# Strassen's seven products for the first MLP layer of the last eight token tiles, and other places for the scores of batches 6 and 7

## The chip, the cores and the metric

One core of a Trainium2 chip. The metric is the time of one execution in device microseconds (us), lower is better. The kernel before took 570.96 us (median of 3 runs, 569.7 to 571.33).

## What is computed

Cosine attention of 8 batches, 12 heads, 448 tokens, 64 channels a head, then a mixer: a low-rank mixing along the tokens and a two-layer MLP, each with its residual.

```python
q_n = q / (norm(q) + 1e-6);  k_n = k / (norm(k) + 1e-6)
attn = softmax(q_n @ k_n.T / tau)
x = (attn @ v), heads side by side          # 8 x 448 x 768
u = x + ((x.T @ U) @ V).T                   # rank 32, along the tokens
out = u + relu(u @ w_ch1) @ w_ch2           # 768 -> 3072 -> 768
```

All inputs and the output are float32; the kernel multiplies in bf16 and accumulates in fp32.

## The kernel before

**Tiles.** The 3584 tokens are 28 tiles of 128. The MLP takes them in order: five units of 3 or 4 tiles (`UNITS`, units 0 to 4, together 16 tiles) by `mlp` (L1085), then the last 12 tiles in six pairs (pairs 0 to 5) by `mlp_seven` (L995). Attention of later batches runs between the matmuls of earlier units. `u` is made per batch in `stage0` (L833); its transpose uT, with channels on the partitions, comes by DMA transposes on SP's queue (`columns_of`, L792).

**A unit.** First layer: for each of 24 blocks of 128 hidden units, six matmuls with a block of w1 as weights and uT as moving data (L1098), into one bank; a ReLU on ACT or DVE (L1121, L1123) writes bf16. Second layer: for each tile and half of the columns, 24 matmuls (L1134), then DVE adds u (L1145), and SP stores the rows.

**A pair.** Its first layer is direct: 12 times two blocks of w1, six matmuls of 256 columns each (L1007), both into one bank, and a ReLU of 512 (L1017, L1019). After every three of the twelve, four DVE sums of 384 (L1029 to L1033) make the combinations of ReLU blocks that Strassen's algorithm (in Winograd's form) needs: S1, S2, S4 and one in place. The second layer then is seven products instead of eight: each 12 matmuls of 384 columns (L1042) with blocks of ReLU, or of their sums, as weights, and blocks of w2, or of their sums, as moving data. The sums of w2 are made once, in `seven_weights` (L965), on DVE (L976). Products share banks and are read in the middle of their accumulation: product 1 is copied out by ACT (L1062); POOL adds three quarters of u to that copy (L1064); DVE adds a bank to such a sum (L1057). Products run in the order 1, 6, 2, 7, 5, 4, 3. A product that goes on in a bank waits for the sum that reads it.

**What sets the order.** Every instruction is an `Op` with an engine, an assumed duration, what it depends on, and the buffers that it acquires and releases (`Slot`, `Ring`; PSUM's eight banks as `BankRing`). `Plan.run` (L156) plays these out with the assumed durations and issues the instructions in the order that results. PE's work lies in streams of fixed order; ACT, DVE and SP take what is ready, by priority; POOL has one queue. On the chip each engine runs its list in this order and waits on semaphores. Where the plan has a gap on PE of more than 0.25 us, it fills it with matmuls on a warm-up tile.

**The scores.** From batch 2 on, scores of a batch come in seven bursts of three (L677): six matmuls on PE (L695; the first burst has twelve of half size), then three exponentials on ACT (L713); `values` (L719) follows as exponentials end. A burst is tied to a place among the matmuls of the MLP: batch b + 2 to the second layer of unit b (`SPOTS`, L1149 to L1154), batch 7 to seven places in pairs 0 and 1 (near L1315). The first burst of a batch needs the transposed keys and queries (qkT) of all six pairs of heads; these come by DMA transposes on SP (L649) into six buffers that the batch before frees burst by burst.

Of the kernel before, what the change touches and what calls it, by code (L numbers as in the profile page):

```python
# [11 lines left out]
FP = mybir.dt.float32  # L12
BF = mybir.dt.bfloat16
AF = mybir.ActivationFunctionType
# [255 lines left out]
def kernel(  # L270
# [12 lines left out]
    nc = tc.nc  # L283

    B, H, S, D = q.shape
    C = H * D
    R = moe_U.shape[-1]
    F = moe_w_ch1.shape[-1]
    NPAIR = H // 2
    CC = C // 128  # L290
    NC = F // 128
    CH = C // 2
    SC = 4
    SCH = S // SC
# [12 lines left out]
    const = ctx.enter_context(tc.tile_pool(name="const", bufs=1))  # L307
# [5 lines left out]
    def fixed(n, shape, dt, name):  # L313

        tiles = [const.tile(shape, dt, name=f"{name}{i}") for i in range(n)]
        return tiles

    def ring(n, shape, dt, name, space=None):
        p = space or pool
        return Ring(n, lambda i: p.tile(shape, dt, name=name, tag=name, bufs=n))  # L320

    def fixed_ring(tiles):
        return Ring(len(tiles), lambda i: tiles[i % len(tiles)])

    HF, QC = NC // 2, 2 * G * SC * D
# [1 line left out]
    ld_t = [qk_t[0:SCH, QC * i:QC * (i + 1)].rearrange("p (i h x) -> p i h x", i=2, h=G) for i in range(3)]  # L327
    xn_t = [qk_t[0:SCH, 3 * QC + 1024 * i:3 * QC + 1024 * (i + 1)].rearrange("p (c x) -> p c x", c=2 * SC)
            for i in range(3)]
    attn_t = fixed(3, [128, SC, 2, 512], BF, "attn")  # L330
    tail_t = [t_[:, SC - 1] for t_ in attn_t]
    v_t = fixed(2, [128, H, SC, D + 8], BF, "v_nat")

# [3 lines left out]
    r_ss = ring(4, [SCH, 2, G, SC], FP, "ss")  # L337
    r_ln = ring(4, [SCH, 2, G, SC], FP, "ln")
    r_inv = ring(4, [SCH, 2, G, SC], FP, "inv")
    r_qkT = ring(6, [128, 2 * SC, SCH], BF, "qkT")  # L340
    r_X = ring(2, [128, 4, C], BF, "X_sb")
    r_A = ring(3, [128, C], BF, "A_sb")
    u_t = const.tile([128, 8, C], BF, name="u_nat")
    r_u = fixed_ring([u_t[:, i, :] for i in range(8)])
# [23 lines left out]
    lead = First()  # L368
    O_t = fixed(3, [128, CH], FP, "O_sb")
    r_O = fixed_ring(O_t)  # L370
    spare = [uT_t[:, CC * 256:].bitcast(FP), relu_t[:, 84 * 128:].bitcast(FP)]
    r_O2 = fixed_ring([x[:, CH * i:CH * (i + 1)] for x in spare for i in range(2)] + O_t)
    r_rd = ring(2, [128, 4, 1], FP, "rd")
    bank_t = psum.tile([128, 8, 512], FP, name="bank")
    banks = Banks(8)
# [1 line left out]
    def bank_ring(groups, cap, shape=None):  # L377
        def make(g):
            if len(g) > 1:
                return bank_t[:, g[0]:g[-1] + 1, :]  # L380
            t_ = bank_t[:, g[0], :]
            if shape is not None:
                t_ = t_[:, 0:shape[0] * shape[1]].rearrange("p (a b) -> p a b", a=shape[0])
            return t_
        return BankRing(banks, groups, cap, make)
# [12 lines left out]
    r_scb = bank_ring([(0, 1), (2, 3)], 2)  # L398
    r_out = bank_ring([(7,), (6,), (5,), (4,)], 4)
    r_warm = bank_ring([(4,)], 1)  # L400
    r_sc1 = bank_ring([(0,), (2,), (1,), (3,)], 4)


# [34 lines left out]
    def pe_t(n):  # L438
        return n / 2400.0 + 0.0025
# [7 lines left out]
    def any_t(n, fast=1, fixed=0.065):  # L447
        return {"ACT": act_t(n), "DVE": dve_t(n, fast, fixed)}
# [333 lines left out]

    class Columns:

        def __init__(self, n):
            self.slot, self.n = Slot(r_uT, NC * CC), n

        @property
        def tile(self):
            return self.slot.tile[:, 0:CC * self.n].rearrange("p (c n) -> p c n", c=CC)  # L790

    def columns_of(tiles):  # L792

        uT = Columns(128 * len(tiles))
        us, ut = [], []
        for i, x in enumerate(tiles):
            u, adds = made[x]
            us.append(u)
            ut.append(plan.add(Op("SP", 0.1, lambda i=i, u=u: nc.sync.dma_start_transpose(
                out=uT.tile[:, :, i * 128:(i + 1) * 128], in_=u.tile),  # L800
                deps=adds, acq=[uT.slot], rel=[u], prio=0, lat=("x", 0.05 * 48, 2.0))))
        return us, uT, ut
# [145 lines left out]
    def store(tile_, c0, c1, O, o):  # L948

        z, t = tile_  # L950
        w = c1 - c0
        for bb in (2 * z, 2 * z + 1):
            o0 = (bb % 2) * S
            lo, hi = max(128 * t, o0), min(128 * (t + 1), o0 + S)
            if lo >= hi:
                continue
            for nn, j, p0, p1 in segments(lo - o0, hi - o0):
                r0 = nn + o0 - 128 * t
                O.uses += 1
                O.left += 1  # L960
                plan.add(Op("SP", 0.1, lambda bb=bb, j=j, p0=p0, p1=p1, r0=r0: nc.sync.dma_start(
                    out=rows(out[bb], j, p0, p1)[:, c0:c1], in_=O.tile[r0:r0 + p1 - p0, 0:w]),
                    deps=[o], rel=[O], prio=2, lat=("x", (p1 - p0) * w * 4 / 200e3, 2.0)))

    def seven_weights(after, qk_free, v_free):  # L965

# [25 lines left out]
                 6: lambda j: T2[:, j], 7: lambda j: B_[:, j, 0, 1]}  # L992
        return right, by

    def mlp_seven(tiles, right, made_by):  # L995

        us, uT, ut = columns_of(tiles)
        rl = relu_t.rearrange("p (x t) -> p x t", t=128)
        Q = rl[:, 0:4 * HF].rearrange("p (j x) t -> p j x t", x=4)
        S1, S2, S4 = [rl[:, 4 * HF + HF * i:4 * HF + HF * (i + 1)] for i in range(3)]  # L1000
        relu = Slot(r_relu, 7)
        tops, ready = [], {}
        for j in range(HF):
            mm = Slot(r_up, 1)
            for e in range(2):
                for cc in range(CC):
                    o = plan.add(Op("PE", pe_t(256), lambda j=j, e=e, cc=cc, mm=mm: nc.tensor.matmul(  # L1007
                        out=mm.tile[:, 256 * e:256 * e + 256], lhsT=w1_sb[:, cc, (2 * j + e) * 128:(2 * j + e + 1) * 128],
                        rhs=uT.tile[:, cc, :], start=(cc == 0), stop=(cc == CC - 1)),
                        deps=ut if cc == 0 else [], acq=[mm] if cc == 0 and e == 0 else [], rel=[uT.slot]), pe_mlp)  # L1010
            tops.append(o)
            r = Op("ACT/DVE", any_t(512), None, deps=[o], acq=[relu], rel=[mm], prio=0)

            def fn(r=r, j=j, mm=mm):
                dst = rl[:, 4 * j:4 * j + 4].rearrange("p x t -> p (x t)")
                if r.by == "ACT":
                    nc.scalar.activation(out=dst, in_=mm.tile[:, 0:512], func=AF.Relu)  # L1017
                else:
                    nc.vector.tensor_relu(out=dst, in_=mm.tile[:, 0:512])  # L1019
            r.fn = fn  # L1020
            ready[j] = {1: plan.add(r)}
            ready[j][2] = ready[j][4] = ready[j][1]
            if j % 3 == 2:
                x = slice(j - 2, j + 1)
                t = 0.06 + 384 * 0.00053

                def sums(f, deps):
                    return plan.add(Op("DVE", t, f, deps=deps, acq=[relu], prio=0.1))
                a = sums(lambda x=x: nc.vector.tensor_add(S1[:, x], Q[:, x, 1], Q[:, x, 3]),  # L1029
                         [ready[i][1] for i in range(j - 2, j + 1)])  # L1030
                c = sums(lambda x=x: nc.vector.tensor_sub(S2[:, x], S1[:, x], Q[:, x, 0]), [a])
                d = sums(lambda x=x: nc.vector.tensor_sub(S4[:, x], Q[:, x, 2], S2[:, x]), [c])
                e_ = sums(lambda x=x: nc.vector.tensor_sub(Q[:, x, 1], Q[:, x, 0], Q[:, x, 1]), [a])  # L1033
                for i in range(j - 2, j + 1):
                    ready[i].update({3: d, 5: a, 6: c, 7: e_})
        left = {1: lambda j: Q[:, j, 0], 2: lambda j: Q[:, j, 2], 3: lambda j: S4[:, j], 4: lambda j: Q[:, j, 3],
                5: lambda j: S1[:, j], 6: lambda j: S2[:, j], 7: lambda j: Q[:, j, 1]}
        line = []
# [1 line left out]
        def product(k, mm, first, last, deps=()):  # L1040
# [5 lines left out]
                    acq=[mm] if first and j == 0 else [], rel=[relu] if j == HF - 1 else []), pe_mlp)  # L1046
            line.append(o)
            return o
        a, b, c = Slot(r_mm, 1), Slot(r_mm, 1), Slot(r_mm, 1)
        s1, y12, y22, y21, o11 = Slot(r_O2, 3), Slot(r_O2, 0), Slot(r_O2, 0), Slot(r_O2, 0), Slot(r_O2, 0)  # L1050
        u1, u2 = us

        def dve(f, deps, acq=(), rel=()):
# [5 lines left out]
        def tile_of(s):  # L1059
            return lambda: s.tile  # L1060
        p1 = product(1, a, True, False)
        cp = plan.add(Op("ACT", 0.42, lambda: nc.scalar.copy(out=s1.tile, in_=a.tile[:, 0:CH]),  # L1062
                         deps=[p1], acq=[s1], prio=-0.5))
        y = [plan.add(Op("POOL", 1.0, lambda y_=y_, u=u, c0=c0: nc.gpsimd.tensor_add(  # L1064
            out=y_.tile, in0=s1.tile, in1=u.tile[:, c0:c0 + CH]), deps=[cp], acq=[y_], rel=[s1, u]), pool_q)
            for y_, u, c0 in ((y12, u1, CH), (y22, u2, CH), (y21, u2, 0))]
        p6 = product(6, b, True, False)
        z12 = dve(bank(tile_of(y12), tile_of(y12), b), [p6, y[0]])
        p2 = product(2, a, False, True, [cp])
# [15 lines left out]
    def mlp(b, tiles, us, uT, ut):  # L1085
# [62 lines left out]
                store(t, c0, c1, O, o)  # L1148

        last_down[b] = [x[-1] for x in downs]  # L1150
        todo = bursts.get(b + 2, ()) if b else ()
        for o, f in zip(bursts.get(2, ()) if b == 1 else (), [0,3,6,9,12,15,18,21]):
            o.deps.append(tops[f])
        spots = [(g, f) for g in range(len(downs)) for f in SPOTS[len(downs)][g]] if todo else ()  # L1154
# [150 lines left out]
    for b, tiles in enumerate(UNITS):  # L1305
# [2 lines left out]
    seven = seven_weights(last_down[len(UNITS) - 1],  # L1308
                          [o for p in range(NPAIR) for o in got[B - 1, p, "qkT"][1]],
                          [last_av[B - 2, p] for p in range(NPAIR)])  # L1310
    hosts = []
    for n in range(0, len(rest), 2):
        hosts.append(mlp_seven(rest[n:n + 2], *seven))
    (t0, l0), (t1, l1) = hosts[:2]
    for o, at in zip(bursts[B - 1], (t0[2], t0[7], l0[0], l0[3], t1[2], t1[7], l1[0])):  # L1315
        o.deps.append(at)

    order = plan.run()
# [44 lines left out]
```

## Time and profile before

| what | value |
|---|---|
| median of three runs | 570.96 us (569.7 to 571.33) |
| the profiled execution, whole | 571.55 us |
| its span, first to last instruction | 569.0 us |
| granted TensorE clock over the span | 0.997 |
| pair 2: first layer, second layer | 15.72 us, 13.65 us |
| L1007, 864 matmuls of 256 columns | 97.6 us busy |
| L1042, second layer of the pairs | 504 matmuls of 384 columns |
| L713, 163 exponentials of 896 | 917 ns each |
| DVE busy, 448 to 569 us | 34.3 of 121 us |
| ACT busy, 448 to 569 us | 30.6 of 121 us |

The profile is one execution. In the view of groups the duration of a matmul includes its way through the array (273 ns for 256 columns), while the next one starts 109 ns later; so lengths of stretches are taken from the chain, and single durations only for the other engines. Start to start is less than the duration on DVE, ACT and POOL too. Lines of the form "start, length, engine, line, operation, out<-in" come from the timeline, with what an engine waited for in square brackets.

### The profile page before, as it was taken

What the parts mean: (1) busy time and instruction counts of PE and PEld (TensorE: products, weight loads), DVE (VectorE), ACT (ScalarE), POOL (GpSimd) and SP (SyncE); (2) the same over time, 40 slices, a digit from 0 to 9 for tenths busy, and PEclk for the clock granted to TensorE, in tenths of its full rate; (3) what the DMA queues carried; (4) which work ended last, traced back from release to release, by engine and by line L of the source; (5) the groups of instructions that cost most, each with busy time, mean ns of one, the idle gap of its engine ahead of it and who ended that gap; (6) DMA issues with size and microseconds to landing.
All of it is one profiled execution on the core that took longest, in us unless ns stands there. A gap on an engine that the chain in (4) does not pass through costs nothing.

```text
span 569.0 us, 12604 instructions
## 1 busy us (share of the span) xinstructions
PE 559.8 (98%) x5207; PEld 362.1 (64%) x5207; DVE 337.8 (59%) x815; ACT 284.5 (50%) x472; POOL 118.1 (21%) x162
## 2 busy tenths in 40 slices
PE   8899999999999999999999999999999999999997
PEld 6565566544565565566556655686786777777784
DVE  7889969987674786477437722479444532323232
ACT  6876645577525672666555546446263231313140
POOL 7626142060041105002300400002001010101001
PEclk9899999999999999999999999999999999999999
DMA  9999999794769649684957714311203111311201
GB/s 152 203 208 136 210 196 137 82 151 76 121 79 151 92 67 113 106 116 52 108 107 131 53 26 85 77 31 31 54 4 43 43 29 56 29 55 29 57 1 55
DMA packets 132665, 50.51 MB, mean 89 GB/s; under 512 B 97760, under 2 KB 132608, under 8 KB 132608
## 3 DMA queue, kind: packets, MB, share of 16 engines
q0 software_dynamic: 72352, 25.73, 40.2%
q1 hardware_dynamic: 60256, 23.98, 21.6%
q8 instruction: 40, 0.66, 0.5%
q14 instruction: 17, 0.14, 0.1%
HBM read 52.02 MB, written 11.01 MB: 111 GB/s over the span
## 4 chain that ended last, share of the span: by engine, by line
PE 94%; DVE 3%; DMA 1%; ACT 1%; issue 0%; POOL 0%; DVEq 0%; ACTq 0%; POOLq 0%
PE bank L1134 22%; PE bank L1098 22%; PE bank L1007 17%; PE bank L1042 14%; PE bank L740 8%; PE bank L695 6%; PE bank L895 2%; DMA qk_all<-in_k_dram 1%; PE bank L488 1%; DVE qk_all L634 1%; ACT attn L708 1%; PE bank L845 1%; DVE X_sb L771 0%; DVE ss L566 0%; DVE ln L586 0%
## 5 line engine op out<-in xcount | busy, mean ns | idle before, releaser
L713 ACT ACTIVATE attn<-bank 128x896 bf16<-128x896 f32 (+1 forms) x163 | 139.2, 917 | 71.7 <-PE bank L695 66.6
L1134 PE MATMUL bank<-w_sb,relu 128*128 128x384 bf16 x768 | 136.3, 326 | 0.0
L1098 PE MATMUL bank<-uT,w_sb 128*128 128x384 bf16 (+1 forms) x720 | 135.3, 337 | 0.0
L1134 PEld LDWEIGHTS <-relu 128*128 128x128 bf16 x768 | 71.0, 98 | 53.4 <-issue 10.7
L1098 PEld LDWEIGHTS <-w_sb 128*128 128x128 bf16 x720 | 67.3, 98 | 54.4 <-issue 6.7
L1007 PE MATMUL bank<-uT,w_sb 128*128 128x256 bf16 x864 | 97.6, 273 | 0.0
L1007 PEld LDWEIGHTS <-w_sb 128*128 128x128 bf16 x864 | 83.8, 98 | 12.4 <-issue 1.8
L1017 ACT ACTIVATE relu<-bank 128x512 bf16<-128x512 f32 x68 | 40.6, 597 | 100.5 <-PE bank L1007 100.5
L1042 PEld LDWEIGHTS <-relu 128*128 128x128 bf16 x504 | 48.7, 98 | 32.4 <-issue 1.4
L1121 ACT ACTIVATE relu<-bank 128x384 bf16<-128x384 f32 (+1 forms) x84 | 42.7, 509 | 48.2 <-PE bank L1098 47.7
L566 DVE TENSOR_REDUCE ss<-sq_all 112x8 f32<-112x512 bf16 x96 | 61.9, 672 | 5.4 <-ACT sq_all L558 5.0
L740 PEld LDWEIGHTS <-attn 128*128 128x128 bf16 (+1 forms) x1536 | 55.0, 98 | 9.1 <-issue 3.5
L634 DVE TENSOR_TENSOR qk_all<-qk_all,inv 112x512 bf16<-112x512 bf16 x93 | 60.7, 680 | 0.1
L740 PE MATMUL bank<-v_nat,attn 128*128 128x65 bf16 (+1 forms) x1536 | 58.1, 194 | 0.8 <-DVE X_sb L771 0.4
L1042 PE MATMUL bank<-w_sb,relu 128*128 128x384 bf16 x288 | 50.4, 326 | 0.0
L1145 DVE TENSOR_TENSOR O_sb<-bank,u_nat 128x384 f32<-128x384 f32 x32 | 17.7, 555 | 51.9 <-PE bank L1134 47.6
L695 PE MATMUL bank<-qkT 64*128 64x448 bf16 (+1 forms) x384 | 47.3, 357 | 1.1 <-ACT qkT L1160 0.5
L510 POOL DMA_DIRECT2D qk_all<-in_q_dram x24 | 17.5, 730 | 141.8 <-ACT attn L713 51.9
L533 POOL DMA_DIRECT2D v_nat<-in_v_dram x42 | 31.0, 744 | 68.7 <-PE bank L740 40.3
L771 DVE TENSOR_TENSOR X_sb<-bank,rd 128x256 bf16<-128x256 f32 x96 | 39.2, 417 | 1.8 <-DVE rd L769 0.2
L1029 DVE TENSOR_TENSOR relu<-relu 128x384 bf16<-128x384 bf16 x24 | 8.6, 357 | 52.5 <-ACT relu L1017 52.3
L558 ACT ACTIVATE sq_all<-qk_all 112x512 bf16<-112x512 bf16 x53 | 31.1, 629 | 7.6 <-DVE ss L566 7.6
(96 smaller groups left out, 419.6 us busy)
## 6 DMA issues: line engine op xcount, KB each, us to landing
qk_all<-in_q_dram POOLq DMA_DIRECT2D x23, 224.0 KB, 5.2
qk_all<-in_k_dram POOLq DMA_DIRECT2D x23, 224.0 KB, 5.8
w_sb<-in_moe_w_ch_dram POOLq DMA_DIRECT2D x4, 1152.0 KB, 17.4
w_sb<-in_moe_w_ch_dram POOLq DMA_DIRECT2D x8, 576.0 KB, 15.8
out_dram<-O_sb SPq DMA_DIRECT2D x14, 168.0 KB, 2.3
v_nat<-in_v_dram POOLq DMA_DIRECT2D x11, 168.0 KB, 7.9
out_dram<-O_sb SPq DMA_DIRECT2D x12, 144.0 KB, 2.1
out_dram<-O_sb SPq DMA_DIRECT2D x11, 120.0 KB, 2.1
```

What stands on the lines that cost most here:

```text
L566: lambda i=i, a0=a0, a1=a1, sq=sq: nc.vector.reduce_sum(ss.tile[:, i, a0:a1, :].rearrange("p h c -> p (h c)"), sq.tile[:, 0:a1 - a0, :].re ...
L634: nc.vector.tensor_mul(dst, src, sc)
L695: nc.tensor.matmul(out=out, lhsT=qkT.tile.rearrange("p b s -> p (b s)")[r, n0:n0 + w], rhs=qkT.tile[r, SC:2 * SC, :].rearrange("p c s -> p ...
L713: exps.append(plan.add(Op("ACT", act_t(2 * S, 0.08), lambda sc=sc, c=c, attn=attn: nc.scalar.activation(out=attn.tile[:, :, off:off + S] i ...
L740: nc.tensor.matmul(out=av.tile[:, t, 0:D + 1], lhsT=tail.tile[:, hh, 128 * t:128 * (t + 1)] if tail and j == SC - 1 else (attn if j < SC - ...
L771: muls.append(plan.add(Op("DVE", dve_t(256), lambda av=av, rd=rd, h=h: nc.vector.tensor_mul(X.tile[:, :, h * D:(h + 1) * D], av.tile[:, :, ...
L1007: o = plan.add(Op("PE", pe_t(256), lambda j=j, e=e, cc=cc, mm=mm: nc.tensor.matmul(out=mm.tile[:, 256 * e:256 * e + 256], lhsT=w1_sb[:, cc ...
L1017: nc.scalar.activation(out=dst, in_=mm.tile[:, 0:512], func=AF.Relu)
L1042: o = plan.add(Op("PE", pe_t(CH), lambda j=j: nc.tensor.matmul(out=mm.tile[:, 0:CH], lhsT=left[k](j), rhs=right[k](j), start=(first and j ...
L1098: o = plan.add(Op("PE", pe_t(n), lambda cc=cc: nc.tensor.matmul(out=mm.tile[:, 0:n], lhsT=w1_sb[:, cc, f * 128:(f + 1) * 128], rhs=uT.tile ...
L1121: nc.scalar.activation(out=relu.tile[:, f, 0:n], in_=mm.tile[:, 0:n], func=AF.Relu)
L1134: nc.tensor.matmul(out=mm.tile[:, 0:c1 - c0], lhsT=relu.tile[:, f, i * 128:(i + 1) * 128], rhs=w2_t[:, f, c0:c1], start=(f == 0), stop=(f ...
```

## The change

**First layer of pairs 2 to 5** (`up_seven`). uT of the pair is split into 2 x 2 (channels, tokens) and w1 into 2 x 2 (channels, hidden units); seven products replace eight. A product is 12 hidden blocks x 3 channel blocks of 128 columns. The blocks lie in three groups of four; a group fills one bank of 512. The products run in the order 1, 6, 2, 7, 5, 3, 4, each over all three groups. Per group: ACT copies product 1 out of its bank; product 2 goes on in that bank, and ACT's ReLU reads it; DVE adds the bank of 6, and of 6 + 7, to the copy, then the banks of 5, 5 + 3 and 6 + 7 + 4 to these; ReLUs of the three that lie in SBUF run on ACT (two) and DVE (one). Four sums of 384 on DVE make the columns' combinations. `sums_of` then makes S1, S2, S4 and the sum in place by groups of 512, S4 of the first two groups on POOL.

**Rows of w1** (`seven_rows`). Twelve DVE sums of 1536, once, into the memory of attention tiles and qkT, which therefore must be done with batch 7; three of the twelve are in place in w1 and wait for the last first-layer matmul of pair 1.

**Second layer of pairs 2 to 5.** The order is 1, 4, 6, 5, 7, 2, 3, with four banks instead of three.

**Scores.** Bursts of batch 6 and 7 get places listed by hand, in both layers of unit 4 and in pair 0.

**Buffers.** The attention tiles, qkT and X_sb become one tile each, cut into views; the spare memory in uT is no longer an output buffer.

```diff
-    attn_t = fixed(3, [128, SC, 2, 512], BF, "attn")
+    attn_all = const.tile([128, 3 * AT], BF, name="attn")
...
-    spare = [uT_t[:, CC * 256:].bitcast(FP), relu_t[:, 84 * 128:].bitcast(FP)]
+    spare = relu_t[:, 84 * 128:].bitcast(FP)
...
+    r_mm4 = bank_ring([(7,), (6,), (5,), (4,), (3,), (2,), (1,), (0,)], 4)
+    r_pure = bank_ring([(7,), (6,), (5,), (4,), (3,), (2,), (1,), (0,)], 8)
...
+    def seven_rows(after, free):
...
+        for i in range(3):
+            A11, A12, A21, A22 = A_[:, i, 0, :, 0], A_[:, i, 1, :, 0], A_[:, i, 0, :, 1], A_[:, i, 1, :, 1]
+            a = rows_(lambda o=S1[i], x=A21, y=A22: nc.vector.tensor_add(o, x, y), free)
+            c = rows_(lambda o=S2[i], x=S1[i], y=A11: nc.vector.tensor_sub(o, x, y), [a])
+            d = rows_(lambda o=S4[i], x=A12, y=S2[i]: nc.vector.tensor_sub(o, x, y), [c])
+            e = rows_(lambda o=A21, x=A11, y=A21: nc.vector.tensor_sub(o, x, y), [a, *after])
+            by[i] = {3: d, 5: a, 6: c, 7: e}
...
+    def up_seven(tiles, relu, tops, ready, left, made_by, x_free):
...
+        a = cols_(lambda: nc.vector.tensor_sub(T(0), U()[:, :, 0, 1], U()[:, :, 0, 0]), ut)
+        c = cols_(lambda: nc.vector.tensor_sub(T(1), U()[:, :, 1, 1], T(0)), [a])
+        d = cols_(lambda: nc.vector.tensor_sub(T(2), U()[:, :, 1, 0], T(1)), [c])
+        e = cols_(lambda: nc.vector.tensor_sub(U()[:, :, 0, 1], U()[:, :, 1, 1], U()[:, :, 0, 1]), [a])
...
+        def product(k, g, mm, first, deps=()):
+            for j in gs[g]:
+                for i in range(3):
...
+                    o = plan.add(Op("PE", pe_t(128), lambda i=i, j=j, jj=jj: nc.tensor.matmul(
+                        out=mm.tile[:, 128 * jj:128 * jj + 128], lhsT=left[k](i, j), rhs=right[k][0](i),
...
+        for k in (1, 6, 2, 7, 5, 3, 4):
+            for g in range(len(gs)):
+                A, B_, C_ = banks_of[g]
...
+                if k == 1:
+                    o = product(1, g, A, True)
+                    x["cp"] = op("ACT", 0.57, lambda g=g, A=A: nc.scalar.copy(out=s1[g].tile, in_=A.tile[:, 0:512]),
...
+                elif k == 6:
+                    o = product(6, g, B_, True)
+                    x["z12"] = op("DVE", PS, sum_op(of(z12[g]), of(s1[g]), B_, False), [o, x["cp"]], [z12[g]])
...
+                elif k == 7:
+                    o = product(7, g, B_, False, [x["z12"]])
...
+                elif k == 5:
+                    o = product(5, g, C_, True)
+                    x["q22"] = op("DVE", PS, sum_op(blocks(g, 3), wide(z22[g]), C_, True), [o, x["z22"]], [relu], [z22[g]])
...
+                elif k == 3:
+                    o = product(3, g, C_, False, [x["q22"]])
...
+                    sums_of(gs[g], relu, ready, [x["r11"]], [x["r12"]], [x["r21"]], [x["r22"]], "POOL" if g < 2 else "DVE")
...
+    def sums_of(js, relu, ready, r11, r12, r21, r22, by="DVE"):
...
+        a = sums(lambda: nc.vector.tensor_add(S1[:, x], Q[:, x, 1], Q[:, x, 3]), [*r12, *r22])
+        c = sums(lambda: nc.vector.tensor_sub(S2[:, x], S1[:, x], Q[:, x, 0]), [a, *r11])
+        e_ = sums(lambda: nc.vector.tensor_sub(Q[:, x, 1], Q[:, x, 0], Q[:, x, 1]), [a], prio=0.15)
+        d = sums(lambda: side.tensor_sub(S4[:, x], Q[:, x, 2], S2[:, x]), [c, *r21], by, prio=0.2)
...
+        if up is not None:
+            d = Slot(r_mm4, 1)
+            p4 = product(4, d, True, True)
+            p6 = product(6, b, True, False)
+            z12 = dve(bank(tile_of(y12), tile_of(y12), b), [p6, y[0]])
+            p5 = product(5, c, True, False)
+            p7 = product(7, b, False, True, [z12])
+            z22 = dve(bank(tile_of(y22), tile_of(y22), b), [p7, y[1]])
+            x22 = dve(bank(tile_of(y22), tile_of(y22), c), [p5, z22])
...
+            p2 = product(2, a, False, True, [cp])
...
+            p3 = product(3, c, False, True, [x22])
+            x12 = dve(bank(tile_of(y12), tile_of(y12), c), [p3, z12], (), [c])
...
-        todo = bursts.get(b + 2, ()) if b else ()
+        todo = bursts.get(b + 2, ()) if 0 < b < 4 else ()
...
+    PURE = 4
...
-        hosts.append(mlp_seven(rest[n:n + 2], *seven))
+        if n // 2 == len(rest) // 2 - PURE:
+            up = seven_rows([hosts[-1][0][-1]], [last_av[B - 1, p] for p in range(NPAIR)])
...
-    for o, at in zip(bursts[B - 1], (t0[2], t0[7], l0[0], l0[3], t1[2], t1[7], l1[0])):
+    for o, at in zip(bursts[B - 2] + bursts[B - 1], [
+            t4[3], t4[10], t4[17], d4[0][0], d4[1][0], d4[2][0], d4[3][0],
+            d4[4][0], d4[5][0], t0[2], t0[7], l0[0], l0[3], l0[5]]):
```

## The prediction

> **What bounds the kernel now.** I read the page first: the share of each engine, then the chain that ended last.
>
> ```profile
> span 569.0 us, 12604 instructions
> PE 559.8 (98%) x5207; PEld 362.1 (64%) x5207; DVE 337.8 (59%) x815; ACT 284.5 (50%) x472; POOL 118.1 (21%) x162
> PE 94%; DVE 3%; DMA 1%; ACT 1%; issue 0%; POOL 0%; DVEq 0%; ACTq 0%; POOLq 0%
> ```
>
> PE is busy for 98% of the span and is 94% of the chain. The chain of its last stretch, in order of time (start, length, what):
>
> ```profile
> 371.45 0.97 PE bank L740 x32
> ...
> 476.64 15.72 PE bank L1007 x144
> 492.36 13.65 PE bank L1042 x84
> 506.01 15.72 PE bank L1007 x144
> ...
> 564.76 0.02 issue
> 564.79 0.56 DVE O_sb L1057
> ```
>
> Each start is the previous start plus its length: PE never pauses here, and the view of waits lists none for PE from 300 us on. So a matmul less shortens the run by its own duration, and a new wait of PE adds its own. One pair of tiles is 15.72 us for the first layer (144 x 109.2 ns) and 13.65 us for the second (84 x 162.5 ns). What else such a pair holds, from the view by windows (PE, PEld, DVE, ACT, POOL busy):
>
> ```profile
> 476.64:506.01 29.37, 29.37 (x230) 22.31 (x229) 8.36 (x22) 7.64 (x13) 2.65 (x3) 1.00 0.24 41
> ```
>
> DVE and ACT are idle for 21 of 29 us: there is room for the new sums, if they come in time.
>
> **What the Trainium skill says.** "TensorE: Matmul & The Clock Gate", section "Back-to-back issue gap", gives two figures for 128 columns: about 56 ns in isolation (N/2.4 + 2.5 ns) and about 81 ns in a real stream of weight load and matmul. The change lives in that gap, so I looked for such streams in the timeline of PE:
>
> ```profile
> 99.77 0.61 PE L488 MATMUL bank<-ident,u_nat 128*128 128x128 bf16 x8
> ...
> 102.30 0.44 PE L895 MATMUL bank<-A_sb,V_sb 128*128 128x128 bf16 x5
> ```
>
> A single one is shown as 0.219 us, so start to start is (0.61 - 0.219)/7 = 55.9 ns and (0.44 - 0.219)/4 = 55 ns, the first with other weights each time. L740 above runs 32 matmuls of 65 columns, each with weights of its own and four in turn into the same bank columns, in 0.97 us: 30 ns. So neither the weight load nor re-accumulating at once binds at 56 ns; the trace disagrees with the 81, and I take 55.9.
>
> "VectorE: DVE Perf Modes", section "The perf-mode tier table": a sum of two bf16 tensors in SBUF runs at 2x, anything out of PSUM at 1x. The trace agrees: 384 bf16 elements take 0.35 us, 384 from a bank 0.56 us (L1057).
>
> "SBUF — State Buffer", section "Who interferes with whom": a DVE instruction with two SBUF inputs contends with a GpSimd instruction that reads SBUF. The timelines of DVE and of POOL show the price:
>
> ```profile
> 387.71 0.69 DVE L1019 TENSOR_SCALAR relu<-bank 128x512 bf16<-128x512 f32 x1
> 388.32 0.75 DVE L976 TENSOR_TENSOR v_nat<-w_sb,qk_all 128x1152 bf16<-128x1152 bf16 x1
> ...
> 394.58 0.35 DVE L1033 TENSOR_TENSOR relu<-relu 128x384 bf16<-128x384 bf16 x1
> 394.85 0.35 DVE L1032 TENSOR_TENSOR relu<-relu 128x384 bf16<-128x384 bf16 x1
> ...
> 396.46 0.75 DVE L976 TENSOR_TENSOR sq_all<-w_sb,qk_all 128x1152 bf16<-128x1152 bf16 x1
> 398.01 0.56 DVE L1057 TENSOR_TENSOR uT<-bank,uT 128x384 f32<-128x384 f32 x1 [0.81 <-POOL uT L1064]
> ```
>
> ```profile
> 395.14 2.84 POOL L1064 TENSOR_TENSOR uT<-uT,u_nat 128x384 f32<-128x384 f32 x1 [68.18 <-ACT uT L1062]
> 397.95 1.78 POOL L1064 TENSOR_TENSOR relu<-uT,u_nat 128x384 f32<-128x384 f32 x2
> ```
>
> POOL's sum takes 0.91 us elsewhere; here 2.84, as it moved only when DVE stopped at 397.21 (it had done some 0.14 us of work in 2.07). POOL stands still while DVE sums pairs in SBUF.
>
> **The change, part by part.**
>
> (1) First layer of four pairs. Out: 144 matmuls of 256 columns, 15.72 us. In: 7 products x 12 blocks x 3 = 252 of 128 columns, 252 x 55.9 = 14.09 us. Gain 1.63 us a pair, 6.53 us in all. The instruction order of the changed kernel holds them (1008 such matmuls, product by product, three groups each). Bounds: 55 ns gives 7.4 us; 81 ns (20.41 us) gives a loss of 18.8 us.
>
> (2) Its sums on DVE and ACT. A product of one group is 12 matmuls, 0.67 us, a step of three 2.01 us. In each step from the second (without product 2) DVE takes three sums of 512 out of banks; such an operation starts 0.61 us after the one before (387.71 to 388.32), 1.83 us a step: DVE keeps pace. The tightest wait: product 3 of a group, in product 5's bank, needs that bank's sum; product 5 ends at 13 x 0.67 = 8.7 us, sum done 9.45, product 3 due 10.05. Product 7 needs product 6's sum: due 6.0, done 3.5. Product 2 needs ACT's copy (about 0.6 us, as L1017): due 4.0, done 1.4. Nothing costs PE time; if DVE fell behind by over 0.6 us, it would.
>
> (3) Sums between the layers, the place I doubt. Let U be the end of the first layer. DVE's order: last bank sum at U+0.05, three ReLUs from U+0.66 (about 0.2 us each, estimated from the 4x row of the tier table and 0.27 us for a 448 copy), then ten bf16 sums of 512 in a row. For 384 the step is 0.27 us (394.58 to 394.85), so 0.34 for 512: from U+1.26 to about U+4.65. The second layer's products (1.95 us each) run 1, 4, 6, 5, 7, 2, 3; product 6 at U+3.9 needs sums done by U+2.4: fine. But POOL must make two S4 sums ahead of its three additions, and it stands still till U+4.65. A 512 bf16 operation takes POOL 1.04 us (L560); less 0.15 done in the gaps, S4 is done at U+6.55, the first addition (0.91) at U+7.45, DVE's sum on it (0.56) at U+8.05 with the signals. Product 7 continues in that sum's bank and is due at U+7.8. PE waits about 0.25 us a pair, 1.0 us in all; all of PE's later products stand behind it. Bounds: none, if POOL gets into more gaps; 0.7 a pair, if S4 runs at POOL's fp32 rate (512/384 x 0.91 = 1.21 us) and the ReLUs take 0.25. Behind product 7 there is room again: the third addition ends near U+10.7, and product 3 (due U+11.7) waits on no addition later than the second.
>
> (4) Row sums of w1: 12 on DVE of 1536 bf16, 0.87 us each (0.67 for 1152, scaled), 10.4 us, in pair 1, where the view by windows (410 to 448 us) has DVE busy for 18.3 of 38 us. First use: product 6 of pair 2, after all but the in-place ones, which product 7 needs 4 us later. Taken at nothing; if pair 1's own sums came late behind them, up to 1 us.
>
> (5) Columns and queues. Four sums of 384 a pair on DVE, during the second layer. They wait for two transposes on SP, which issue at U and land by U+5 (2.54 us of queue, 3.3 to landing); DVE reaches them at U+8. SP's stores stand behind these as before. No price.
>
> (6) The scores of batches 6 and 7. No instruction is added: 14 bursts on PE, 42 exponentials on ACT, and what they free (key transposes on SP, values, projections). Up to PE row 6295 both orders agree, in instructions and in waits. Adding durations from there, batch 7's first burst comes some 7.5 us earlier, its last transpose stands behind two stores of unit 4's fourth half-tile and lands some 10 us ahead of use. The next four bursts stand some 4.4 us apart; 3 exponentials take 2.54 us, so ACT has time, and DVE takes seven ReLUs, nine weight sums and 16 others, 15.3 us in a stretch of 17. Four banks in flight (5 us of matmuls) cover it. I take 0; bounds 0 and 1.5 us. Before, the densest such stretch (DVE 25.4 of 35 us) cost PE nothing.
>
> (7) The tail is unchanged: product 3, one addition, two stores.
>
> **Sum.** The profiled execution took 571.55 us (span 569.0, 2.55 around it): 571.55 - 6.53 + 1.0 = 566.0. It lies 0.59 above the median of the runs, 570.96; on that base 570.96 - 5.55 = 565.4.
>
> **The rivals.**
> A, likeliest: as summed, 565.4.
> B: no wait at product 7, every sum hidden: 570.96 - 6.5 = 564.4. For it: DVE's pace and gaps are estimates with an error as large as the wait. Against: the 2.84 us addition.
> C: longer waits, 0.6 to 1.6 us a pair at product 7, or the moved scores filling ACT and DVE: 567 to 571. For it: every new sum stands in one DVE queue. Against: margins of 0.5 us and more nearly everywhere.
> D, slower: the weight load sets the pace of 128-column matmuls. Place: L1066 of the changed kernel; at 81 ns 570.96 + 18.8 = 589.8. It decides from 15.72/252 = 62.4 ns, above which the change loses. Against it: 55.9 and 30 ns above.
> That the change doesn't do what it says is excluded by the order of instructions.
>
> **How the numbers follow.** A 0.47, B 0.27, C 0.19, D 0.07. Half of C lies below 568.6. The range 563.6 to 568.6 holds A, B (runs before lay up to 1.3 below their median) and that half: 0.83. A measurement of this kernel can tell about 0.3%, 1.7 us: faster is A, B and C below 569.2, 0.88; same is the rest of C, 0.05; slower D, 0.07.
>
> **What would show it.** A first layer of a late pair of 14.1 us in the chain (right), or its matmuls 62 ns apart (D). PE idle before product 7 of the second layer, released by DVE, 0.2 to 0.4 us, four times; POOL's first S4 sum about 3 us long. Waits of PE on ACT or DVE in unit 4 or pair 0 would prove part 6 wrong, waits inside the products of the first layer part 2.

## The result, and the profile after

The changed kernel takes 566.37 us (median of 4 runs, 565.53 to 566.71) against 570.38 us for the kernel before on the same chip: a ratio of 0.9926, with a 95% interval of 0.9906 to 0.9947. It is faster by 4.0 us, where 5.55 us were predicted. Taken again on another occasion it gave 565.98 us, ratio 0.9934 [0.9919, 0.9950].

The profiled execution of the changed kernel took 565.53 us. Its page, the same three lines as shown of before (span; busy time of each engine; shares of the chain that ended last):

```profile
span 563.8 us, 13573 instructions
...
PE 552.9 (98%) x5639; PEld 361.0 (64%) x5639; DVE 395.4 (70%) x901; ACT 282.1 (50%) x466; POOL 135.2 (24%) x170
...
PE 84%; DVE 9%; issue 2%; POOL 1%; ACT 1%; POOLq 1%; DMA 1%; DVEq 0%
```

PE is busy 6.9 us less and is still the bound, but its share of the chain has fallen from 94% to 84%: the chain now leaves PE somewhere. (The two spans differ by 5.2 us; 1.5 of it is there when the first long stretch of MLP matmuls begins, at 41.29 us before and 39.77 after, and stays the same until the change begins. In a second execution of the changed kernel that stretch begins at 41.76, so the 1.5 us belong to the executions and not to the change.) The chain of waits shows where it leaves PE, here around the end of pair 3's first layer (start, length, what):

```profile
468.13 6.01 PE bank L1196 x36
474.14 6.71 PE bank L1066 x120
...
489.46 0.75 DVE relu L1148 x2
...
493.87 1.15 POOL relu L1151
495.02 0.88 POOL qkT L1219
495.92 0.57 DVE qkT L1212
496.53 6.01 PE bank L1196 x36
```

Read from the bottom: PE's product 7 starts at 496.53, released by DVE's sum at L1212, which waited for POOL's first addition at L1219, which stood behind POOL's second S4 sum at L1151; and that leads back to DVE's pair sums. Not all of the 9% that the chain gives to DVE is lost time: farther back in it stand DVE's sums out of the banks (L1088), which ran while PE was busy. The view of PE's waits from 300 us on (us in total, times, longest) has nothing else in it:

```profile
PE bank L1196 <- DVE qkT L1212: 1.0, 2, 0.5
PE bank L1196 <- DVE relu L1212: 0.5, 1, 0.5
PE bank L1196 <- DVE O_sb L1212: 0.5, 1, 0.5
```

Four waits, one for each pair with the new first layer, and all the same one. PE's timeline of pair 3 (start, length, operation, count, idle before in brackets) gives the two numbers that the prediction turned on:

```profile
473.98 2.17 PE L1066 MATMUL bank<-uT,w_sb 128*128 128x128 bf16 x36
...
488.05 2.11 PE L1196 MATMUL bank<-w_sb,relu 128*128 128x384 bf16 x12
...
496.53 3.73 PE L1196 MATMUL bank<-w_sb,relu 128*128 128x384 bf16 x22 [0.52 <-DVE qkT L1212]
```

The first layer runs from 473.98 to 488.05: 14.07 us for 252 matmuls, 55.8 ns each, without a pause. Product 7 was due four products of 12 x 162.5 ns after 488.05, at 495.85, and starts at 496.53: 0.68 us late. The row shows 0.52, because the matmul before it is still passing through the array when the next could have started; what the pair loses is the 0.68. The window of a whole pair says the same, 28.40 us where the matmuls alone are 14.07 + 13.65 = 27.72:

```profile
468.13:496.53 28.40, 27.88 (x336) 22.28 (x336) 19.56 (x40) 7.81 (x13) 7.03 (x6) 1.00 0.17 43
```

So the sum of the change as measured is four pairs x (15.72 - 14.07 - 0.68) = 3.9 us, close to the 4.0 us between the medians.

### The profile page after: what moved, and what is told of

The parts are those of the page before. It is cut to its first block, busy times and chain, and to the rows that moved or that the text cites. A ratio compares the mean times of both kernels' runs of the same rounds, so it can differ in the third digit from the quotient of the medians.

```text
span 563.8 us, 13573 instructions
## 1 busy us (share of the span) xinstructions
PE 552.9 (98%) x5639; PEld 361.0 (64%) x5639; DVE 395.4 (70%) x901; ACT 282.1 (50%) x466; POOL 135.2 (24%) x170
## 4 chain that ended last, share of the span: by engine, by line
PE 84%; DVE 9%; issue 2%; POOL 1%; ACT 1%; POOLq 1%; DMA 1%; DVEq 0%
PE bank L1309 23%; PE bank L1273 23%; PE bank L1196 9%; PE bank L754 8%; PE bank L709 6%; PE bank L1167 6%; PE bank L1066 5%; DVE relu L1088 4%; PE bank L909 2%; DVE v_nat L1088 1%; PE bank L502 1%; POOL relu L1151 1%; ACT attn L722 1%; PE bank L859 1%; POOLq L1543 1%
## 5 line engine op out<-in xcount | busy, mean ns | idle before, releaser
L1273 PEld LDWEIGHTS <-w_sb 128*128 128x128 bf16 x720 | 67.1, 98 | 54.8 <-issue 7.4
L1296 ACT ACTIVATE relu<-bank 128x384 bf16<-128x384 f32 (+1 forms) x80 | 40.8, 511 | 46.4 <-PE bank L1273 46.0
L1151 POOL TENSOR_TENSOR relu<-relu 128x512 bf16<-128x512 bf16 x8 | 17.2, 2170 | 88.2 <-ACT qkT L1217 42.7
L783 DVE RECIPROCAL rd<-bank 128x4 f32<-128x4 f32 x96 | 16.5, 176 | 27.7 <-PE bank L754 26.8
L1298 DVE TENSOR_SCALAR relu<-bank 128x384 bf16<-128x384 f32 (+1 forms) x40 | 23.3, 584 | 16.9 <-PE bank L1273 16.4
L1066 PE MATMUL bank<-uT,w_sb 128*128 128x128 bf16 x576 | 34.1, 219 | 0.0
```

What stands on the lines that cost most here:

```text
L1066: o = plan.add(Op("PE", pe_t(128), lambda i=i, j=j, jj=jj: nc.tensor.matmul(out=mm.tile[:, 128 * jj:128 * jj + 128], lhsT=left[k](i, j), r ...
L1273: o = plan.add(Op("PE", pe_t(n), lambda cc=cc: nc.tensor.matmul(out=mm.tile[:, 0:n], lhsT=w1_sb[:, cc, f * 128:(f + 1) * 128], rhs=uT.tile ...
L1296: nc.scalar.activation(out=relu.tile[:, f, 0:n], in_=mm.tile[:, 0:n], func=AF.Relu)
```

## The experiments

**The theory** after this reading: the gain is the matmuls' own time, and what is missing from it is the chain from DVE's pair sums by way of POOL's two S4 sums to product 7. **Rivals**: DVE's own queue is what comes late, so that moving S4 to DVE makes it worse; the new places of the scores are the real gain, or hide a loss; part of the gain comes once and not by pairs. None of these kernels leaves out any part of the computation.

**The changed kernel again**, as the base for the next three on the same chip.

> The changed kernel as it is, on the chip of the next three. Expected 0.9926 of the kernel before (566.2 us if that takes 570.4), with PE waiting some 0.5 us before product 7 of the second layer, four times.

Measured 565.98 us (565.59 to 567.51), before 570.16 there, with the same four waits of 0.5 us in the view of PE's waits.

**S4 on DVE alone.**

```diff
-                    sums_of(gs[g], relu, ready, [x["r11"]], [x["r12"]], [x["r21"]], [x["r22"]], "POOL" if g < 2 else "DVE")
+                    sums_of(gs[g], relu, ready, [x["r11"]], [x["r12"]], [x["r21"]], [x["r22"]], "DVE")
```

> All three S4 sums of a late pair on DVE, none on POOL. Theory (POOL stands still during DVE's ten sums, then makes two S4 sums before the addition that product 7 waits for): POOL's first addition ends some 6.4 us after the first layer, DVE's sum on it at 7.0, product 7 is due at 7.8, so all four waits go: 2.7 us less than the changed kernel, about 563.6 us. Rival (DVE's own queue between the layers is what is late, POOL only happens to end last): DVE gets 0.34 us more for each of two sums, the waits grow by 0.7 us a pair: 2.7 us more, about 569.

Measured 563.06 us (562.82 to 563.38), ratio to before 0.9877 [0.9858, 0.9896]: 2.9 us under the changed kernel, where its waits were 4 x 0.68 = 2.7 us. PE waits for nothing from 300 us on, and the chain of its last stretch is PE alone:

```profile
473.84 14.07 PE bank L1066 x252
487.91 13.65 PE bank L1196 x84
501.56 14.07 PE bank L1066 x252
515.63 13.65 PE bank L1196 x84
```

DVE has 8 sums more and nothing is late for it: its own queue was not the bound. POOL's timeline shows that the contention is still there, and no longer matters:

```profile
490.45 5.17 POOL L1219 TENSOR_TENSOR qkT<-qkT,u_nat 128x384 f32<-128x384 f32 x3 [22.55 <-ACT qkT L1217]
```

Three additions of 0.91 us last 5.17 us, the first of them held up for some 2.5 us by DVE's sums. But it is done by about 493.85 (the end of the row, 495.62, less two additions of 0.88), DVE's sum on it runs at 493.86, when product 6 is out of the array, which it needs in any case, and product 7 is due at 495.54. By its median this is the fastest version of the study, faster than both kernels; the next one is 0.1% behind it.

**S4 stays on POOL, but behind its additions.** Nothing changes but the order in POOL's queue.

```diff
-        d = sums(lambda: side.tensor_sub(S4[:, x], Q[:, x, 2], S2[:, x]), [c, *r21], by, prio=0.2)
+        d = Op(by, t if by == "DVE" else 0.2 + len(js) * 128 * 0.0022, lambda: side.tensor_sub(S4[:, x], Q[:, x, 2], S2[:, x]),
+               deps=[c, *r21], acq=[relu], prio=0.2)
+        if by == "POOL":
+            behind.append(d)
+        else:
+            plan.add(d)
...
+        for o in behind:
+            plan.add(o, pool_q)
+        behind.clear()
```

> Same work on the same engines, only POOL's order: the three additions of u first, the two S4 sums behind them. Theory: product 7's wait goes, as in the run before, and product 3 (due 11.7 us after the first layer) still finds S4, which should be done at about 11.2: 2.7 us less than the changed kernel, about 563.6; if S4 is later than that, PE waits before product 3 instead, by up to 1 us a pair. Rival (DVE's queue): DVE's work is the same, so the wait stays and the time is that of the changed kernel, 566.3.

Measured 563.57 us (563.18 to 564.03), ratio 0.9886 [0.9870, 0.9903], and no wait of PE. POOL does the same five operations in the other order:

```profile
491.21 4.65 POOL L1224 TENSOR_TENSOR qkT<-qkT,u_nat 128x384 f32<-128x384 f32 x3 [20.66 <-ACT qkT L1222]
495.83 2.49 POOL L1151 TENSOR_TENSOR relu<-relu 128x512 bf16<-128x512 bf16 x2
```

With the S4 work left on POOL and only its place changed, the loss is gone. So it is the queue order on POOL, and not the S4 work as such. POOL's standing still, which makes the order matter, is read from the timelines; it is there in all four versions (S4 on both, on DVE, behind, on POOL), and no run takes it away.

**All three S4 sums on POOL**, the opposite dose.

```diff
-                    sums_of(gs[g], relu, ready, [x["r11"]], [x["r12"]], [x["r21"]], [x["r22"]], "POOL" if g < 2 else "DVE")
+                    sums_of(gs[g], relu, ready, [x["r11"]], [x["r12"]], [x["r21"]], [x["r22"]], "POOL")
```

> The suspected cost increased: all three S4 sums on POOL. Theory: POOL's chain before the first addition is 1.15 us longer and starts 0.34 us earlier, the wait of product 7 grows by 0.8 us a pair: 3.2 us more than the changed kernel, about 569.5. Rival (DVE's queue): DVE has 0.34 us less, the wait shrinks: about 565.

Measured 570.98 us (569.86 to 572.89), ratio 1.0017 [1.0010, 1.0025]: 5.0 us over the changed kernel, so the whole gain of the new first layer is gone. The sign and the place are as the theory has them (the view of PE's waits holds only product 7: 1.9 us in pairs 2 to 4, and 1.3 in the last pair); the size is larger than expected. DVE's timeline before product 7 of pair 3 shows why:

```profile
494.88 0.35 DVE L1048 TENSOR_TENSOR uT<-uT 128x384 bf16<-128x384 bf16 x1
495.27 1.19 DVE L1049 TENSOR_TENSOR uT<-uT 128x384 bf16<-128x384 bf16 x1
496.39 1.30 DVE L1051 TENSOR_TENSOR uT<-uT 128x384 bf16<-128x384 bf16 x1
497.61 1.31 DVE L1050 TENSOR_TENSOR uT<-uT 128x384 bf16<-128x384 bf16 x1
```

The columns' sums now come ahead of the awaited one. Three of them take 1.2 to 1.3 us instead of 0.35, for each waits for a whole instruction of POOL, which is at its S4 sums; and POOL's three take 5.58 us instead of 3 x 1.15: at first it stands still for DVE's pair sums, as in the other versions, and then it waits for the columns' sums in turn. This delays S4, the additions behind it, and product 7. The last pair is the check on it, for no pair follows, so there are no columns' sums in the way. POOL's S4 sums in pairs 3 and 5:

```profile
493.13 5.58 POOL L1151 TENSOR_TENSOR relu<-relu 128x512 bf16<-128x512 bf16 x3 [21.49 <-ACT qkT L1217]
...
552.71 5.07 POOL L1151 TENSOR_TENSOR relu<-relu 128x512 bf16<-128x512 bf16 x3 [21.49 <-ACT qkT L1217]
```

In the last pair product 7 starts 1.45 us after it is due, close to what the theory has (0.68 + 0.8); in the three others it is 2.07. The 0.6 us between them goes with the columns' sums.

**The changed kernel with the old places of the scores.**

```diff
-        todo = bursts.get(b + 2, ()) if 0 < b < 4 else ()
+        todo = bursts.get(b + 2, ()) if b else ()
...
-    t4, d4 = anchors[4]
-    for o, at in zip(bursts[B - 2] + bursts[B - 1], [
-            t4[3], t4[10], t4[17], d4[0][0], d4[1][0], d4[2][0], d4[3][0],
-            d4[4][0], d4[5][0], t0[2], t0[7], l0[0], l0[3], l0[5]]):
+    for o, at in zip(bursts[B - 1], (t0[2], t0[7], l0[0], l0[3], t1[2], t1[7], l1[0])):
```

> The changed kernel with the places of the scores of before (batch 6 in the second layer of unit 4, batch 7 at seven places in pairs 0 and 1). Theory: the moved scores gain PE nothing by themselves; they empty the attention memory early enough for the row sums of w1. With the old places batch 7's values end in the second layer of pair 1, and by the order of instructions nine of the twelve row sums and the sums for batch 7's u stand in one run on DVE at the start of pair 2. From the last of its mixer matmuls, 39 matmuls (2.2 us) into pair 2, DVE still has the end of that run before it: eight sums of 0.87 us and six of 0.5, of which some 3 us can be done before. Product 6 of pair 2 waits some 5 us (3 to 7): 571 us (569 to 573), with waits of PE on DVE at L1066 in pair 2 only, and pairs 3 to 5 as in the changed kernel. Rival: the places are free, the row sums fit anywhere: 566, no wait in pair 2.

Measured 574.67 us (574.46 to 575.97), ratio to before 1.0078 [1.0064, 1.0092]: slower than before, and 1.44% or 8.2 us over the changed kernel by the two ratios. The view of PE's waits has, beside 0.2 us for a sum of batch 7's u at the same place, one line that the changed kernel lacks, with the expected place and size:

```profile
PE bank L1066 <- DVE attn L1026: 4.7, 2, 4.2
```

But 4.9 us of waits do not make 8.2. PE's timeline and the windows from the first stop on (columns as before; the last but two is the granted clock) show the rest:

```profile
448.15 0.22 PE L1066 MATMUL bank<-uT,attn 128*128 128x128 bf16 x1
448.49 0.79 PE L909 MATMUL bank<-A_sb,V_sb 128*128 128x384 bf16 x2
449.83 0.23 PE L1066 MATMUL bank<-uT,attn 128*128 128x128 bf16 x1 [0.55 <-DVE attn L1026]
450.29 0.32 PE L909 MATMUL bank<-A_sb,V_sb 128*128 128x384 bf16 x1 [0.23 <-DVE u_nat L923]
454.82 3.81 PE L1066 MATMUL bank<-uT,attn 128*128 128x128 bf16 x34 [4.20 <-DVE attn L1026]
458.42 4.67 PE L1066 MATMUL bank<-uT,w_sb 128*128 128x128 bf16 x72
```

```profile
448.15:454.82 6.67, 1.42 (x7) 0.31 (x5) 6.64 (x11) 0.58 (x1) 0.00 (x0) 0.83 0.06 18
454.82:458.42 3.60, 3.60 (x35) 3.60 (x36) 2.97 (x4) 0.00 (x0) 0.00 (x0) 0.50 0.00 0
458.42:462.93 4.51, 4.51 (x74) 4.51 (x73) 1.83 (x3) 1.79 (x3) 0.00 (x0) 0.89 0.14 29
```

After 4.2 us of idleness the granted clock is 0.50, and the 34 matmuls take 3.60 us, 106 ns each instead of 55.8. The mean of 0.89 in the last window makes some 1.0 us at half clock there, so the clock is full again some 4.6 us after the restart. The two rows from 454.82 on, 106 matmuls, take 8.11 us instead of 5.92: 2.2 us more. The layer as a whole takes 23.31 us (445.65 to 468.96), of which 14.07 are its own and 1.0 are six mixer matmuls between. Of the 8.2 left, the half clock is 2.2, and 6.1 lie between 448.15 and 454.82, where PE starts five matmuls that take 0.6 us at full pace. The view of waits shows 4.9 of these 6.1, because it counts a stop only from when the matmul before it has left the array, and leaves out two short ones of 0.1 us. The estimate of the wait was right and the time came out beyond its range, for neither the clock nor this difference was in it.

The Trainium skill, "TensorE: Matmul & The Clock Gate", section "What's actually happening", says that PE drops to half its clock after an idle window of about 3.4 us and needs about as long of work to get it back. These traces agree in that the stop of 4.2 us ends at half clock, which took 4.6 us of work to go, and that the 1.9 us stops of the version with all S4 on POOL did not bring it about (granted clock 1.00 in the 1.67 us after one). They do not show that a stop below 3.4 us is safe. The mean of 0.83 in the first window makes some 2.3 us at half clock, so the clock fell near 452.6, about 2.0 us after the last matmul; but PE had run only five matmuls since 448.15.

**The kernel before with only the new places** (the same lines as above, the other way round, on the kernel before).

```diff
-        todo = bursts.get(b + 2, ()) if b else ()
+        todo = bursts.get(b + 2, ()) if 0 < b < 4 else ()
...
-    for o, at in zip(bursts[B - 1], (t0[2], t0[7], l0[0], l0[3], t1[2], t1[7], l1[0])):
+    t4, d4 = anchors[4]
+    for o, at in zip(bursts[B - 2] + bursts[B - 1], [
+            t4[3], t4[10], t4[17], d4[0][0], d4[1][0], d4[2][0], d4[3][0],
+            d4[4][0], d4[5][0], t0[2], t0[7], l0[0], l0[3], l0[5]]):
```

> The kernel before with nothing changed but the places of the scores of batches 6 and 7. Theory (part 6 of the prediction): no instruction more or less, no new wait of PE: 570.4, ratio 1.000 within 0.3%. Rivals: the move costs up to 1.5 us by itself (572), which the first layer's gain would have hidden; or it gains something itself (569 or less), which would have been put down to Strassen's algorithm.

Measured 570.01 us (569.46 to 571.23) against 570.20, ratio 0.9997 [0.9989, 1.0005], and PE waits for nothing from 300 us on. By itself the move is worth nothing in either direction. The two runs together say what it is for: it lets batch 7's values finish with the attention memory before pair 2, so that the row sums of w1, which are written there, can be made in pair 1.

**The dose: two pairs instead of four**, on the version with S4 on DVE.

```diff
-    PURE = 4
+    PURE = 2
```

> The version with S4 on DVE alone, with the new first layer in the last two pairs instead of four. Theory: with no wait left, each pair is worth its matmuls, 15.72 - 14.07 = 1.65 us: two pairs fewer cost 3.3 us against 563.1, 566.4 in all (565.8 to 567), and pairs 2 and 3 are 29.37 us, pairs 4 and 5 27.72. Rival: a part of the gain is got once, from the order around the change (places, buffers, row sums), and not by pairs: below 565, or above 568 if the later row sums and columns collide with the direct pairs.

Measured 566.82 us (566.49 to 567.79), ratio 0.9941 [0.9929, 0.9954]; 3.3 us more than with four pairs were expected, and the difference of the ratios, 0.64% of 570.2 us, is 3.6 us, with some 1 us of uncertainty by the two intervals. The chain holds two pairs of each kind, with nothing between:

```profile
475.70 15.72 PE bank L1167 x144
491.42 13.65 PE bank L1196 x84
505.07 14.07 PE bank L1066 x252
519.14 13.65 PE bank L1196 x84
```

The gain goes by pairs, 1.65 us each; within that uncertainty no part of it is got once.

## Why the prediction was right, and where it was not

The time lies in the range, and the mechanism is the forecast one: a gain by the matmuls, less a wait at product 7. The forecast of 565.4 stood on a median before of 570.96; here it was 570.38. The gain fell short of its sum by 1.55 us, and the lower base gave 0.6 of that back.

- **(1) First layer.** Right: 14.07 us against 14.09, 55.8 ns against 55.9. The dose shows the same 1.65 us a pair. This also rules out D: the weight loads do not set the pace of matmuls of 128 columns here. Taking the trace's 55.9 ns rather than the 81 ns of the Trainium skill's page was what this prediction rested on.
- **(2) Sums within the first layer.** Right: no wait of PE at L1066 in the changed kernel. The step of 0.61 us is right too: the ReLU behind the last bank sum starts 0.61 us after it (488.25 to 488.86 in the rows below). The bank sums themselves start 0.67 us apart, but that is PE's pace, 12 x 55.8 ns a product, and not DVE's.
- **(3) Sums between the layers.** This is the step that was mis-sized. The mechanism is as foretold, and S4's two versions above show it as a cause: POOL stands still while DVE sums pairs, S4 comes before the additions in POOL's queue, product 7 waits. The wait was put at 0.25 us a pair and is 0.68. POOL's timeline and DVE's, with U = 488.05:

```profile
490.72 4.30 POOL L1151 TENSOR_TENSOR relu<-relu 128x512 bf16<-128x512 bf16 x2 [21.38 <-ACT qkT L1217]
494.98 2.76 POOL L1219 TENSOR_TENSOR qkT<-qkT,u_nat 128x384 f32<-128x384 f32 x3
```

```profile
484.90 4.04 DVE L1088 TENSOR_TENSOR relu<-bank,X_sb 128x512 bf16<-128x512 f32 x6
488.86 0.69 DVE L1122 TENSOR_SCALAR relu<-relu 128x512 bf16<-128x512 bf16 x3
489.46 0.75 DVE L1148 TENSOR_TENSOR relu<-relu 128x512 bf16<-128x512 bf16 x2
...
492.48 0.41 DVE L1151 TENSOR_TENSOR relu<-relu 128x512 bf16<-128x512 bf16 x1
495.92 0.56 DVE L1212 TENSOR_TENSOR qkT<-bank,qkT 128x384 f32<-128x384 f32 x1 [3.02 <-POOL qkT L1219]
```

DVE's ten sums end at U + 4.84, not 4.65 (+0.19). They began 0.15 later, as did the last bank sum: the prediction has it at U + 0.05, as if a matmul's result were there when the next matmul starts, but a matmul of 128 columns is shown as 0.22 us and the next one starts after 0.056; the sum starts at U + 0.20 (six sums 0.67 apart from 484.90). S4 is done at U + 6.97, 2.13 us after that instead of 1.90 (+0.23): one such sum takes 1.15 us on POOL, where I had taken 1.04 from another 512 bf16 operation. The addition and DVE's sum were right within 0.03 us, and PE starts 0.04 us after it. Together 0.43 us a pair, 1.7 us in all: the whole shortfall. The upper bound in the text, 0.7 a pair, lay nearer than the value taken, though its reasons were only in part these; each error was small, but the wait is a difference of two times near U + 8, so two errors of 0.2 us nearly tripled it.
- **(4) Row sums of w1.** The size was right (they start 0.87 us apart), and they cost nothing where they stand. But "taken at nothing" is only true with part 6: with the old places eight of the twelve stand on DVE in pair 2, among the sums of batch 7's u, and the run takes 8.2 us more.
- **(5) Columns and queues.** Right for the changed kernel: DVE reaches them at U + 8.35 and nothing waits for them. With all S4 on POOL they came ahead of the awaited sum and had a price.
- **(6) Moved scores.** Right: nothing, shown by the kernel before with the new places only. What the prediction left unsaid is that parts 4 and 6 are one edit: the move has no price and no gain, and is the condition for the row sums' price of nothing.
- **(7) Tail.** Unchanged, as said.

B, no wait at product 7, did not happen, and is what S4 on DVE makes of the kernel: 563.06 us, with the forecast for B at 564.4. C began at waits of 0.6 us a pair: with 0.68 the changed kernel is just in C by its waits, so C, given 0.19, came nearer to what happened than A, given 0.47. The time, 566.37 us, lies 1.0 above A's 565.4 and 0.6 below the 567 at which C begins; on the base of 570.38 C would begin at 566.4. The range holds the time on either base, since it took in half of C: that is owed to its width and not to the sum of A.

## What to carry to other kernels

When work is taken off the bounding engine and given to helpers, follow the helpers' queues up to the next instruction of the bounding engine that waits for them, and look at what stands ahead of that in each queue: here the optional work (S4, due much later) stood in front of the urgent addition, and changing that order alone was worth 2.4 us. Where a forecast is a wait of a few tenths of a microsecond between two times of several, small errors in one direction add up to more than the wait: count the time until a result has left the array, and take the price of each step from the same operation at the same size where the trace has it. An edit that costs nothing may be what makes another cost nothing; undo it alone in both kernels before calling it neutral.

## What was not expected of the hardware

- **The contention of DVE and POOL goes both ways.** The Trainium skill, "SBUF — State Buffer", section "Who interferes with whom", calls their shared ports an exclusive lock. While DVE ran its pair sums back to back, POOL hardly moved: the two S4 sums that began at 490.72 took 4.30 us instead of 2.30, and POOL got on only after DVE's last sum. But once POOL is running, DVE's sum of 384 waits for a whole POOL instruction and takes up to 1.31 us instead of 0.35, as above. DVE's sums of a bank and a buffer were not slowed (0.56 us at 495.92, beside POOL's additions). Why the side that holds the lock changes at some moments and not at others wasn't tried.
- **A stop of 4.2 us of PE costs more than itself**: the half clock that follows added 2.2 us over 106 matmuls; stops of 1.9 us cost only themselves. The clock fell about 2.0 us into the long stop, behind a stretch in which PE had little to do.
- **POOL's sum of 512 bf16 takes 1.15 us**, no faster by element (2.25 ns) than its fp32 sum of 384 (0.88 us start to start, 2.3 ns).
